# Attention state of a linear-attention + gated-FFN kernel: read-out in four 64x64 array tiles, update by single heads in column tiles directly behind AV

## The chip, the cores and the metric

The kernel runs on one core of a Trainium2 chip. The metric is device time in microseconds (us), the median of a kernel's runs.

Names used below: PE is the TensorE matmul engine, DVE is VectorE, ACT is ScalarE, POOL is GpSimd (it issues most loads), SP is SyncE. A matmul's "tile" is the part of the PE array that it uses, written rows*columns.

## The reference

Four batches, eight heads, 768 positions, head size 64. Each head keeps a 64x64 state that decays by its own factor `lam`.

```python
for b in range(nb):                      # blocks along the sequence
    intra = einsum('bhic,bhjc->bhij', qb, kb) * Dmask      # scores, masked by powers of lam
    intra = einsum('bhij,bhjd->bhid', intra, vb)           # "AV"
    inter = einsum('bhid,bhde->bhie', qb * lam_pow, kv_state)   # state read-out
    out[:, :, sl] = intra + inter
    kv_state = lam_block * kv_state + einsum('bhsd,bhse->bhde', kb * rev_pow, vb)   # state update
x = out as (tokens, 512)
y = (sigmoid(x @ w_gate) * (x @ w_val)) @ w_out            # 512 -> 1536 -> 512
```

## The kernel before

It takes the sequence in six steps of 128 positions. In each step PE makes 12 FFN *units* (four gate matmuls `gp` and four value matmuls `vp` each) and then four blocks of output matmuls (`po`). The attention of the next step is threaded in behind those units: scores `sp`, masked by DVE into `MT`; then the read-out and AV, both summed into `op`; `op` is copied to `XT`, which the next gate and value matmuls read. ACT makes the sigmoid `sg`, DVE the product `ht`, and PE's `po` reads `ht`.

The attention's state `Sb` is held as block-diagonal 128x128 matrices, one per batch and head pair, so that one full-array matmul serves two heads. Half of each is zeros.

```python
Sb = stp.tile([128, B, HP, 128], BF16)               # HP = 4 head pairs

def piece_kd(n, hs):                                  # scale K for the update, on ACT
    for h in hs:
        nc.scalar.mul(KD[n][:, :, h, :], T_["k", n][:, :, h, :], kds[:, h:h + 1])

def piece_a(n, bs):
    for b in bs:
        OP[n, b] = ps_at.tile([128, HP, C], FP32)
        for hp in range(HP if n > 0 else 0):          # read-out, full array, 16 a step
            nc.tensor.matmul(OP[n, b][:, hp, :], lhsT=Sb[:, b, hp, :], rhs=QS[n, b][:, hp, :], ...)
    for b in bs:                                      # AV, 128x64 column tiles, 32 a step
        for hp in range(HP):
            for u in range(2):
                us = slice(u * 64, (u + 1) * 64)
                nc.tensor.matmul(OP[n, b][us, hp, :], lhsT=T_["v", n][:, b, 2 * hp + u, :],
                                 rhs=MT[n, b][:, u, hp, :], ...)

def piece_c(n, hps):                                  # update, full array, two calls of 8 a step
    for hp in hps:
        cp = ps_at.tile([128, B, 128], FP32)
        for b in range(B):
            nc.tensor.matmul(cp[:, b, :], lhsT=KD[n][:, b, 2 * hp:2 * hp + 2, :],
                             rhs=T_["v", n][:, b, 2 * hp:2 * hp + 2, :], ...)
        for u in range(2):                            # only the diagonal blocks are used
            us = slice(u * 64, (u + 1) * 64)
            ...                                       # Sb = dec * Sb + cp, 64x256 each, on DVE
# ... behind units 0 and 1 of steps 2, 3, 4; in step 1 directly behind AV
more[0] = [pair(piece_c, n, 0)]
more[1] = [pair(piece_c, n, 1)]
```

The first step works the same way while the weights are still being loaded.

## Time and profile before

| | before |
|---|---|
| time, median of runs | 232.66 us (232.62 to 232.94) |
| span in the profile | 231.2 us |
| PE busy | 96% |
| first gate matmul | 16.52 us |
| step period (read-out to read-out) | 35.53 us |

How to read it: PE has almost no room left, so only two things can shorten the kernel: a shorter sequence of matmuls, or a gap in it that closes. The page of the profile says both in three lines (span; busy time, share and instruction count of each engine; shares of the chain of work that ended last, where "issue" is time in which an engine waited for nothing that the profile shows and a q behind a name is that engine's queue).

```profile
span 231.2 us, 3734 instructions
PE 221.5 (96%) x1483; PEld 110.6 (48%) x1508; DVE 109.5 (47%) x183; ACT 92.8 (40%) x175; POOL 47.0 (20%) x55
...
PE 78%; DMA 13%; DVE 3%; POOL 3%; issue 2%; POOLq 0%
```

The groups that the change touches, by line and shape (busy us, mean ns of one, then idle time before them). The full-array read-out and update, the DVE update, and ACT's scaling of K:

```profile
L98 ACT ACTIVATE kd<-kb,kds 128x256 bf16<-128x256 bf16 x40 | 17.8, 497 | 0.0
L260 DVE SCALAR_TENSOR_TENSOR Sb<-Sb,dec,cp 64x256 bf16<-64x256 bf16 x32 | 15.3, 478 | 0.8
L252 PE MATMUL cp<-vb,kd 128*128 128x128 bf16 x80 | 5.9, 219 | 0.1
L230 PE MATMUL op<-QS,Sb 128*128 128x128 bf16 x80 | 5.3, 219 | 0.0
```

PE's busy figures mislead here, because the records of pipelined matmuls overlap (219 ns each for 128x128, started 56 ns apart). Starts are what count. The timeline of PE (columns: start us, busy us, engine, line, operation, tensors, array tile, shape, count, and in brackets the idle time before with what ended it) gives the wait for a slice of WV at 38.29; the attention of step 1 (41.55 to 44.55) with a stop of PE at 49.25; and the attention of step 3 (112.86 to 114.87) with its update behind units 0 and 1:

```profile
10.85 0.62 PE L178 MATMUL tq<-ident,qb 128*128 128x128 bf16 x8 [0.39 <-DMA qb<-in_q_dram]
...
16.52 1.02 PE L273 MATMUL gp<-XT,WG 128*128 128x512 bf16 x4 [0.34 <-DVE XT L246]
...
38.29 1.04 PE L279 MATMUL vp<-XT,WV 128*128 128x512 bf16 x4 [0.33 <-DMA WV<-in_moe_w_val_dram]
...
41.55 1.06 PE L230 MATMUL op<-QS,Sb 128*128 128x128 bf16 x16
42.53 1.08 PE L236 MATMUL op<-MT,vb 128*64 128x128 bf16 x32
43.55 1.07 PE L252 MATMUL cp<-vb,kd 128*128 128x128 bf16 x16
44.55 1.02 PE L273 MATMUL gp<-XT,WG 128*128 128x512 bf16 x3
...
49.25 1.02 PE L279 MATMUL vp<-XT,WV 128*128 128x512 bf16 x4 [0.22 <-DVE ht L282]
...
112.86 1.06 PE L230 MATMUL op<-QS,Sb 128*128 128x128 bf16 x16
113.85 1.08 PE L236 MATMUL op<-MT,vb 128*64 128x128 bf16 x32
114.87 10.53 PE L290 MATMUL po<-WO,ht 128*128 128x512 bf16 x47
...
126.97 0.61 PE L252 MATMUL cp<-vb,kd 128*128 128x128 bf16 x8
```

Differences of starts in step 3: read-out 0.99 us, AV 1.02 us. An update of eight matmuls, from its start to the next gate matmul, takes 0.44 us (126.97 to 127.41), twice per step. Counts such as x47 instead of x48, or x3 instead of x4, are records missing from the trace, not missing work.

The DVE updates cost PE more than their matmuls. The chain of waits around unit 4 of step 3 (start us, us, what), before:

```profile
130.61 0.88 PE vp L279 x4
...
131.51 0.48 DVE Sb L260
...
132.01 0.49 DVE Sb L260
...
132.53 0.70 DVE ht L282
...
133.27 1.02 PE gp L273 x4
```

DVE is still updating the state when the value product of the last unit is ready; `ht` comes late, its PSUM tile comes free late, and the next gate matmul starts 1.09 us after the last value group (132.18 to 133.27) instead of the usual 0.86. So 0.23 us are lost in each of steps 2, 3 and 4.

### The profile page before, as it was taken

Reading aid. Unit: us, or ns where it says so; the run is one execution under the profiler, and the core shown is the slowest. Engines: PE = TensorE matmul, PEld = TensorE weight load, DVE = VectorE, ACT = ScalarE, POOL = GpSimd, SP = SyncE. Lnnn points to the kernel's source line nnn. Section 1 sums busy time; section 2 is a strip of 40 time slices with the busy share of each in tenths; the row PEclk is TensorE's granted clock in tenths of the full one; section 3 lists DMA queues with packets and bytes.
Section 4 is the critical chain, followed back from the end, with each engine's and each line's share of the span. In section 5 each row is a group of like instructions: output and inputs, shape, how many; then the busy total and the mean of one; then the engine's idle time right before and its main releaser. Section 6 shows DMA issues by size and latency. Waiting matters only on the chain.

```text
span 231.2 us, 3734 instructions
## 1 busy us (share of the span) xinstructions
PE 221.5 (96%) x1483; PEld 110.6 (48%) x1508; DVE 109.5 (47%) x183; ACT 92.8 (40%) x175; POOL 47.0 (20%) x55
## 2 busy tenths in 40 slices
PE   6889999999999999999999999999999999999993
PEld 2544555644444644444644544644544554444442
DVE  3963668971068401978300978400778600333300
ACT  5557347532225823347433327442333342433220
POOL 7977672000530080026000030000000000000000
PEclk9999999999999999999999999999999999999999
DMA  7999999999799889969922967012100002100022
GB/s 114 156 176 195 173 173 176 207 168 174 209 166 164 170 94 189 224 129 114 157 53 108 209 43 52 1 45 94 45 0 0 3 35 101 48 0 0 0 91 93
DMA packets 103473, 25.15 MB, mean 109 GB/s; under 512 B 93600, under 2 KB 100512, under 8 KB 103456
## 3 DMA queue, kind: packets, MB, share of 16 engines
q0 software_dynamic: 80992, 13.90, 77.0%
q1 hardware_dynamic: 22320, 11.01, 18.5%
q8 instruction: 12, 0.20, 0.3%
q14 instruction: 5, 0.04, 0.0%
q10 hardware_dynamic: 144, 0.00, 0.0%
HBM read 28.32 MB, written 6.29 MB: 150 GB/s over the span
## 4 chain that ended last, share of the span: by engine, by line
PE 78%; DMA 13%; DVE 3%; POOL 3%; issue 2%; POOLq 0%
PE po L290 27%; PE vp L279 22%; PE gp L273 21%; DMA WV<-in_moe_w_val_dram 10%; DMA vb<-in_v_dram 3%; PE op L236 2%; PE sp L216 2%; DVE Sb L260 2%; PE op L230 2%; PE cp L252 2%; DVE ht L282 1%; POOL qb L78 1%; POOL vb L78 0%; POOL kb L78 0%; POOL WV L85 0%
## 5 line engine op out<-in xcount | busy, mean ns | idle before, releaser
L282 DVE TENSOR_TENSOR ht<-sg,vp 128x512 bf16<-128x512 bf16 x72 | 49.4, 687 | 102.6 <-PE vp L279 101.0
L279 PE MATMUL vp<-XT,WV 128*128 128x512 bf16 x282 | 73.4, 379 | 1.0 <-DMA WV<-in_moe_w_val_dram 0.3
L273 PE MATMUL gp<-XT,WG 128*128 128x512 bf16 x277 | 72.8, 379 | 0.9 <-DVE XT L246 0.3
L276 ACT ACTIVATE sg<-gp 128x512 bf16<-128x512 f32 x72 | 43.0, 597 | 74.1 <-PE gp L273 72.0
L290 PE MATMUL po<-WO,ht 128*128 128x512 bf16 (+1 forms) x294 | 62.7, 370 | 0.4 <-issue 0.2
L279 PEld LDWEIGHTS <-WV 128*128 128x128 bf16 x288 | 28.0, 98 | 34.8 <-DMA WV<-in_moe_w_val_dram 0.9
L290 PEld LDWEIGHTS <-ht 128*128 128x128 bf16 x300 | 29.0, 98 | 32.5
L273 PEld LDWEIGHTS <-WG 128*128 128x128 bf16 x288 | 26.8, 98 | 31.4 <-issue 1.8
L295 ACT COPY ob<-po 128x512 f32<-128x512 f32 (+1 forms) x24 | 13.9, 578 | 45.7 <-PE po L290 45.7
L224 DVE TENSOR_TENSOR MT<-sp,mask 128x512 bf16<-128x512 f32 x48 | 30.4, 682 | 0.6 <-PE sp L216 0.5
L98 ACT ACTIVATE kd<-kb,kds 128x256 bf16<-128x256 bf16 x40 | 17.8, 497 | 0.0
L260 DVE SCALAR_TENSOR_TENSOR Sb<-Sb,dec,cp 64x256 bf16<-64x256 bf16 x32 | 15.3, 478 | 0.8
L361 POOL COPY gates<-kt 128x1 bf16<-128x1 bf16 x4 | 0.8, 188 | 69.9 <-DMA kt<-kb 69.9
L246 ACT CAST XT<-op 128x512 bf16<-128x512 f32 x21 | 11.0, 596 | 7.1 <-PE op L236 7.0
L78 POOL DMA_DIRECT2D qb<-in_q_dram x8 | 11.5, 1441 | 3.5 <-issue 1.6
L78 POOL DMA_DIRECT2D vb<-in_v_dram x7 | 10.7, 1533 | 2.6 <-issue 1.4
L78 POOL DMA_DIRECT2D kb<-in_k_dram x7 | 10.2, 1459 | 1.5 <-DMA WV<-in_moe_w_val_dram 0.7
L304 PE MATMUL zps<-Sb 128*128 128x512 bf16 x22 | 7.8, 482 | 2.1 <-DVE Sb L123 2.1
L236 PE MATMUL op<-MT,vb 128*64 128x128 bf16 x192 | 7.1, 221 | 0.4 <-DVE MT L224 0.4
L236 PEld LDWEIGHTS <-vb 128*64 128x64 bf16 x192 | 5.7, 109 | 1.6 <-DMA vb<-in_v_dram 0.4
L252 PEld LDWEIGHTS <-kd 128*128 128x128 bf16 x80 | 5.1, 98 | 2.0
L252 PE MATMUL cp<-vb,kd 128*128 128x128 bf16 x80 | 5.9, 219 | 0.1
(42 smaller groups left out, 77.3 us busy)
## 6 DMA issues: line engine op xcount, KB each, us to landing
out_dram<-ob SPq DMA_DIRECT2D x23, 256.0 KB, 2.0
vb<-in_v_dram POOLq DMA_DIRECT2D x5, 512.0 KB, 7.9
kb<-in_k_dram POOLq DMA_DIRECT2D x4, 512.0 KB, 10.6
qb<-in_q_dram POOLq DMA_DIRECT2D x4, 512.0 KB, 12.7
WO<-in_moe_w_out_dram POOLq DMA_DIRECT2D x2, 768.0 KB, 16.7
WG<-in_moe_w_gate_dram POOLq DMA_DIRECT2D x5, 256.0 KB, 9.6
WV<-in_moe_w_val_dram POOLq DMA_DIRECT2D x5, 256.0 KB, 10.2
qb<-in_q_dram POOLq DMA_DIRECT2D x4, 256.0 KB, 8.4
```

What stands on the lines that cost most here:

```text
L78: nc.gpsimd.dma_start(out=T_[c, n][:, b0:b1], in_=src[b0:b1, :, sl, :].rearrange("b h s d -> s (b h) d"))
L98: nc.scalar.mul(KD[n][:, :, h, :], T_["k", n][:, :, h, :], kds[:, h:h + 1])
L224: nc.vector.tensor_tensor(out=MT[n, b][:, u], in0=SP[n, b][u], in1=mask[:, u], op=ALU.mult)
L236: nc.tensor.matmul(OP[n, b][us, hp, :], lhsT=T_["v", n][:, b, 2 * hp + u, :], rhs=MT[n, b][:, u, hp, :], start=(n == 0 and hp == 0), stop= ...
L252: nc.tensor.matmul(cp[:, b, :], lhsT=KD[n][:, b, 2 * hp:2 * hp + 2, :], rhs=T_["v", n][:, b, 2 * hp:2 * hp + 2, :], start=(b == 0), stop=( ...
L260: nc.vector.scalar_tensor_tensor(out=Sb[us, :, hp, us], in0=Sb[us, :, hp, us], scalar=dec[us, hp:hp + 1], in1=cp[us, :, us], op0=ALU.mult, ...
L273: nc.tensor.matmul(gp, lhsT=WG[:, mt, fs], rhs=x[:, mt, :], start=(mt == 0), stop=(mt == NMT - 1))
L276: nc.scalar.activation(sg, gp, AF.Sigmoid)
L279: nc.tensor.matmul(vp, lhsT=WV[:, mt, fs], rhs=x[:, mt, :], start=(mt == 0), stop=(mt == NMT - 1))
L282: nc.vector.tensor_mul(HT[n, ft], sg, vp)
L290: nc.tensor.matmul(po[:, :c1 - c0], lhsT=HT[n, ft][:, tt * 128:(tt + 1) * 128], rhs=WO[:, ft, c0:c1], start=(ft == 0), stop=(ft == NFT - 1))
L295: nc.scalar.copy(ob[:, c0:c1], po[:, :c1 - c0])
```

## The change

Its intent: do no work on zeros. The state is stored compactly (`[128, HP, B, 64]`). The read-out becomes 32 matmuls in 64x64 tiles, four of them side by side. The update becomes 32 matmuls of 128x64 column tiles, with two head pairs in one PSUM tile, and is moved right behind AV, so that the DVE updates run under the 10 us of `po` matmuls.

For four 64x64 tiles to be busy at once, two of them have to take their rows from one half of the partitions and write to the other half (diag below is the run without it). The change gets these by swapping the two heads of every pair in batches 2 and 3. This swap is made where q and k are loaded (from step 1 on), and so it needs swapped copies of two small tables, a swapped choice of mask, and loads split into three.

```diff
+    def swapped(n, b):
+        return n > 0 and b >= NB2
+    def slot(n, b, h):
+        return h ^ 1 if swapped(n, b) else h
+    def half(b, h):
+        return (1 - h % 2) if b >= NB2 else h % 2
 ... (in load)
+            nat = b1 if n == 0 or c == "v" else min(b1, NB2)
+            if b0 < nat:
+                nc.gpsimd.dma_start(out=T_[c, n][:, b0:nat], in_=src[b0:nat, :, sl, :]...)
+            if nat < b1:
+                for u in range(2):
+                    nc.gpsimd.dma_start(out=T_[c, n][:, m:b1, u::2, :],
+                                        in_=src[m:b1, 1 - u::2, sl, :]...)
 ... (in piece_kd: one ACT operation per head and half of the batches, for n > 0)
-            nc.scalar.mul(KD[n][:, :, h, :], T_["k", n][:, :, h, :], kds[:, h:h + 1])
+            for bs in ((0, B),) if n == 0 else ((0, NB2), (NB2, B)):
+                i = slot(n, bs[0], h)
+                nc.scalar.mul(KD[n][:, at, i, :], T_["k", n][:, at, i, :], kds[:, h:h + 1])
 ...
-    Sb = stp.tile([128, B, HP, 128], BF16, tag="Sb", name="Sb")
+    Sb = stp.tile([128, HP, B, 64], BF16, tag="Sb", name="Sb")
 ...
+    lamqs = const.tile([128, HP, C], BF16, tag="lamqs")
+    decs = const.tile([128, HP], FP32, tag="decs")
 ... (in tables_late)
+        for o, i in ((lamqs, lamq), (decs, dec)):
+            for u in range(2):
+                nc.sync.dma_start(out=o[rows_of(u)], in_=i[rows_of(1 - u)])
 ...
+    def piece_i(n):
+        for b in range(B):
+            OP[n, b] = ps_at.tile([128, HP, C], FP32, name="op", tag="ps")
+        for i in range(NB2):
+            for hp in range(HP):
+                for u, b in ((0, i), (1, NB2 - 1 - i), (0, NB2 + i), (1, B - 1 - i)):
+                    w = u if b < NB2 else 1 - u
+                    nc.tensor.matmul(OP[n, b][rows_of(w), hp, :], lhsT=Sb[rows_of(u), hp, b, :],
+                                     rhs=QS[n, b][rows_of(u), hp, :], ...)
 ... (in piece_c)
-            cp = ps_at.tile([128, B, 128], FP32, name="cp", tag="ps")
+        cp = ps_at.tile([128, len(hps), B, 64], FP32, name="cp", tag="ps")
+                for w in range(2):
+                    h = 2 * hp + w
+                    nc.tensor.matmul(cp[rows_of(half(b, h)), i, b, :],
+                                     lhsT=KD[n][:, b, slot(n, b, h), :], rhs=T_["v", n][:, b, h, :], ...)
+            for at, d in ((slice(0, NB2), dec), (slice(NB2, B), decs)):   # 128x128 on DVE
+                nc.vector.scalar_tensor_tensor(out=Sb[:, hp, at, :], in0=Sb[:, hp, at, :], ...)
 ... (in att)
+            piece_i(n)
             piece_a(n, range(B))
             piece_x(n, range(B))
+            if n < NSTEP - 1:
+                piece_c(n, [0, 1])
+                piece_c(n, [2, 3])
 ...
-                more[0] = [pair(piece_c, n, 0)]
-                more[1] = [pair(piece_c, n, 1)]
```

## The prediction

> **What bounds it.** PE: busy 96% of the 231.2 us span at full granted clock (first two parts of the page), 78% of the chain of waits; DMA is 13%, all before 38.3 us (last: 0.33 us of PE idle for the last WV slice). From then on PE is almost gapless, so only what shortens PE's sequence, or an idle gap in it, counts. DVE (47%), ACT (40%) and POOL have room. Per step the timeline of PE shows: state read-out 16 matmuls, 0.98 us; AV 32 matmuls, about 1.02 us; state update 2x8 matmuls, 0.44 us each; the other 33 us are gate, value and output matmuls, which the change doesn't touch.
>
> **Read-out (5 steps).** Single matmul starts in the trace: 128x128 full-array ones follow every 56 ns; AV's column tiles and the scores' row tiles start in pairs 3 ns apart, pairs every 56 ns. So tiles do run side by side. Four 64x64 tiles: 32 matmuls in 8 groups, about 8x56 = 0.45 us instead of 0.89. A change of array shape costs: from the last full-array matmul's slot to the first tiled one and back I read 93-95 ns each time. The Trainium skill (TensorEngine Tiling, Key Properties) says that a mode switch drains the array; this trace agrees. The change adds one switch per step (full to 64x64) and about 25 ns for a first weight load. Net saving about 0.32 us a step.
>
> **Update (5 steps).** 16x56 = 0.89 us becomes 16 pairs with 64 moving columns: 28 ns a pair if weight loads hide. The trace shows column-tile weight loads 27 ns apart at AV's start, so hiding is marginal; I estimate 32 ns, 0.50 us. Right behind AV it needs no new switch, except at step 0 (+0.19 us). Saving 0.39 us at steps 2-4, 0.2 at step 0 (which the WV wait at 38 us mostly swallows).
>
> **DVE waits.** State updates behind units 0 and 1 delay ht and stop PE 0.23 us at unit 4 of steps 2, 3, 4 (97.7, 133.3, 168.8 us) and 0.22-0.38 us at 49.2. They move under the 10 us of output matmuls, and 8x507 ns becomes, by my estimate, 8x370 ns. Those four stops should go: 0.9-1.05 us.
>
> **Costs.** The scaling of K becomes 16 ACT operations per step instead of 8 (pitch 0.40 us each becomes about 0.30, as the 128-column table exponentials show): a unit's ACT work reaches 1.7 of 1.73 us, still hidden, except at step 1: there read-out waits for the mask products (all four op banks are wanted at once; DVE ends them at 42.5), and the second update tile waits for ACT's backlog. Step 1 gains nothing and may lose 0.2 us. Loads of k and q split in three: POOL issues longer[...]. The queue is saturated then (DMA share 9 tenths), so I expect 0, at worst 0.8 us. Four small table copies: nothing.
>
> **Sum.** 4x0.32 + 3x0.39 + 1.0 - 0.1 = about 3.4 us: 232.7 becomes 229.3 us, range 228.3 to 230.9. Faster by over 2% (under 228.0) 7%, within 2% 91%, slower 2%.
>
> **What would show it.** Read-out stage (first read-out to first AV matmul) near 0.55 us, groups of four starts; update 32 matmuls near 0.5 us; no PE stop at unit 4 of steps 2-4; state-update DVE ops near 370 ns pitch; step period from 35.53 us (112.86 to 148.40) to about 34.6; first 38 us unchanged within 0.5.
>
> **What would make it wrong.** Four tiles that don't overlap (read-out stays 0.9; then 230.6); short column-tiled matmuls bound by their weight loads at 55 ns a pair (update stays 0.9; 230.5); the last WV slice landing late; ACT lag stopping sigmoid, hence PE, in units 6 to 9.

## The result, and the profile after

| | before | after |
|---|---|---|
| time, median of runs | 232.66 us (232.62 to 232.94) | 230.25 us (230.21 to 230.28) |
| ratio | | 0.9894, interval 0.9877 to 0.9911 |
| span | 231.2 us | 228.4 us |
| PE busy | 96% | 96% |

A ratio here and below is the mean time of one kernel's fast runs over that of the other's of the same rounds, so it is not quite the ratio of the quoted medians. The kernel became 2.4 us faster, 1.1%, where 3.4 us had been expected. The measured time lies inside the predicted range.

The page after (span; engines; chain):

```profile
span 228.4 us, 4108 instructions
PE 218.3 (96%) x1642; PEld 107.2 (47%) x1668; DVE 100.9 (44%) x177; ACT 98.2 (43%) x207; POOL 57.9 (25%) x73
...
PE 89%; DVE 3%; DMA 3%; issue 2%; POOL 1%; POOLq 0%; DVEq 0%
```

DVE gave up 8.6 us of work and ACT took on 5.4; neither is the bottleneck. The groups after, by line and shape, answer to the four of before:

```profile
L121 ACT ACTIVATE kd<-kb,kds 128x128 bf16<-128x128 bf16 x64 | 20.1, 390 | 0.0
L300 DVE SCALAR_TENSOR_TENSOR Sb<-Sb,dec,cp 128x128 bf16<-128x128 bf16 x16 | 5.5, 342 | 3.2 <-PE cp L291 3.2
...
L291 PE MATMUL cp<-vb,kd 128*64 128x64 bf16 x160 | 3.6, 196 | 0.1
L262 PE MATMUL op<-QS,Sb 64*64 64x128 bf16 x160 | 3.6, 219 | 0.4 <-DVE MT L252 0.4
```

The timeline of PE after, same columns: prologue, step 1, step 3.

```profile
12.09 0.62 PE L206 MATMUL tq<-ident,qb 128*128 128x128 bf16 x8 [1.06 <-DMA qb<-in_q_dram]
...
17.82 1.02 PE L313 MATMUL gp<-XT,WG 128*128 128x512 bf16 x4 [0.34 <-DVE XT L283]
...
42.47 0.40 PE L262 MATMUL op<-QS,Sb 64*64 64x128 bf16 x3
43.25 0.60 PE L262 MATMUL op<-QS,Sb 64*64 64x128 bf16 x29 [0.38 <-DVE MT L252]
43.78 1.08 PE L273 MATMUL op<-MT,vb 128*64 128x128 bf16 x32
44.70 0.93 PE L291 MATMUL cp<-vb,kd 128*64 128x64 bf16 x32
45.81 1.04 PE L313 MATMUL gp<-XT,WG 128*128 128x512 bf16 x3 [0.18 <-DVE XT L283]
...
112.91 0.64 PE L262 MATMUL op<-QS,Sb 64*64 64x128 bf16 x32
113.48 1.08 PE L273 MATMUL op<-MT,vb 128*64 128x128 bf16 x32
114.39 0.67 PE L291 MATMUL cp<-vb,kd 128*64 128x64 bf16 x32
115.00 4.71 PE L330 MATMUL po<-WO,ht 128*128 128x512 bf16 x20
```

Step 3 did what was hoped: read-out 0.57 us (112.91 to 113.48) instead of 0.99, update 0.61 us (114.39 to 115.00, with the switch back to the full array) instead of 2 x 0.44, and no stop at unit 4. Step 1 did not: its read-out is cut in two by a wait for the mask products. And the first gate matmul comes 1.30 us later.

Cutting the two timelines at the same places gives the balance (starts of the first matmul of each stage; differences in us):

| stage | before | after | change |
|---|---|---|---|
| start to first gate matmul | 16.52 | 17.82 | +1.30 |
| first gate to read-out of step 1 | 25.03 | 24.65 | -0.38 |
| read-out of step 1 to its first gate | 3.00 | 3.34 | +0.34 |
| that gate to the first output matmul | 7.29 | 6.92 | -0.37 |
| first output matmul to read-out of step 2 | 25.49 | 25.58 | +0.09 |
| periods, steps 2 to 5 (three) | 3 x 35.53 | 3 x 34.59 | 3 x -0.94 |
| read-out of step 5 to the last output block | 33.10 | 32.68 | -0.42 |
| sum | 217.03 | 214.77 | -2.26 |

The sum is that of the PE timeline; the median time differs by 2.41 us, and the two executions that were profiled (232.94 and 230.23 us; the first is the longest of its four) by 2.71. What lies behind the start of the last matmul varied between the profiled executions from 5.1 to 5.8 us, without a reason that I found. Differences in total time under about 0.5 us are therefore read from the stages, not from the totals. Two stages scatter, too, as each kernel has one profile: the first gate matmul of move_col came 0.36 us later than before, although nothing ahead of it is changed, and the last WV slice landed at 37.67 us in out_swap and at 38.18 in out_swap_x, whose loads are the same.

Two readings explain most of this table without an experiment:

- *Period.* 0.94 us is read-out 0.33 (0.99 minus 0.57, less 0.09 for the added switch of array shape), update 0.39 (AV and update together 1.02 + 0.89 before, 0.91 + 0.61 after) and the stop of 0.23 us at unit 4. The single matmul starts in the trace show why: the 64x64 matmuls start in groups of four, 3 to 4 ns apart, with groups 55 to 56 ns apart; the update's column tiles start in pairs 31.7 ns apart.
- *Step 1.* The read-out took 1.31 us there (42.47 to 43.78), AV 0.92, the update with its waits 1.11.

The second needs the other engines. ACT, timeline after (the scalings of K, a sigmoid between them):

```profile
38.92 1.27 ACT L121 ACTIVATE kd<-kb,kds 128x128 bf16<-128x128 bf16 x4
40.10 0.58 ACT L316 ACTIVATE sg<-gp 128x512 bf16<-128x512 f32 x1
...
43.39 1.27 ACT L121 ACTIVATE kd<-kb,kds 128x128 bf16<-128x128 bf16 x4
```

DVE, timeline after, the product that waits for this sigmoid and the mask products behind it:

```profile
40.71 0.69 DVE L322 TENSOR_TENSOR ht<-sg,vp 128x512 bf16<-128x512 bf16 x1 [1.18 <-PE sp L244]
41.32 2.48 DVE L252 TENSOR_TENSOR MT<-sp,mask 128x512 bf16<-128x512 f32 x4
```

Four half scalings take 1.27 us where two whole ones took 0.91. The sigmoid behind them therefore starts late (40.10, right when they end), `ht` starts at 40.71, and the mask products end near 43.8. The bracket names PE as the releaser of `ht`, but the scores it names had started at 40.09; the sigmoid ended at 40.68 and is the one that came last. The read-out needs all four output tiles at once, and these come free only as DVE finishes with the scores. The last scalings of K begin at 43.39 and keep ACT until about 44.6. Its first copy to `XT`, which frees a PSUM tile, therefore ends only at 45.13, and the second half of the update waits for that: 0.26 us between single starts at 44.92 and 45.18. In later steps the same scalings stand in units with room (ACT is idle 1.1 us before the last sigmoid of step 2).

What needed experiments is the prologue, and the question which part of the change earns the period.

### The profile page after: what moved, and what is told of

The parts are those of the page before. It is cut to its first block, busy times and chain, and to the rows that moved or that the text cites. A ratio compares the mean times of both kernels' runs of the same rounds, so it can differ in the third digit from the quotient of the medians.

```text
span 228.4 us, 4108 instructions
## 1 busy us (share of the span) xinstructions
PE 218.3 (96%) x1642; PEld 107.2 (47%) x1668; DVE 100.9 (44%) x177; ACT 98.2 (43%) x207; POOL 57.9 (25%) x73
## 4 chain that ended last, share of the span: by engine, by line
PE 89%; DVE 3%; DMA 3%; issue 2%; POOL 1%; POOLq 0%; DVEq 0%
PE po L330 27%; PE vp L319 27%; PE gp L313 27%; DMA qb<-in_q_dram 3%; PE sp L244 3%; PE op L273 2%; DVE MT L252 2%; PE op L262 1%; PE cp L291 1%; DVE XT L283 1%; PE tq L206 1%; POOL kb L92 0%; PE tk L206 0%; DVE QS L213 0%; POOL qb L92 0%
## 5 line engine op out<-in xcount | busy, mean ns | idle before, releaser
L316 ACT ACTIVATE sg<-gp 128x512 bf16<-128x512 f32 x72 | 42.9, 596 | 66.0 <-PE gp L313 63.3
L121 ACT ACTIVATE kd<-kb,kds 128x128 bf16<-128x128 bf16 (+1 forms) x72 | 23.7, 402 | 0.0
L98 POOL DMA_DIRECT2D qb<-in_q_dram x10 | 9.0, 916 | 3.1 <-DMA vb<-in_v_dram 2.1
L98 POOL DMA_DIRECT2D kb<-in_k_dram x10 | 8.9, 902 | 1.0 <-DMA WG<-in_moe_w_gate_dram 0.6
L92 POOL DMA_DIRECT2D qb<-in_q_dram x7 | 8.4, 1202 | 0.8 <-POOLq L517 0.8
L92 POOL DMA_DIRECT2D kb<-in_k_dram x6 | 7.0, 1166 | 0.0
L300 DVE SCALAR_TENSOR_TENSOR Sb<-Sb,dec,cp 128x128 bf16<-128x128 bf16 x16 | 5.5, 342 | 3.2 <-PE cp L291 3.2
```

What stands on the lines that cost most here:

```text
L92: nc.gpsimd.dma_start(out=T_[c, n][:, b0:nat], in_=src[b0:nat, :, sl, :].rearrange("b h s d -> s (b h) d"))
L98: nc.gpsimd.dma_start(out=T_[c, n][:, m:b1, u::2, :], in_=src[m:b1, 1 - u::2, sl, :].rearrange("b h s d -> s (b h) d"))
L121: nc.scalar.mul(KD[n][:, at, i, :], T_["k", n][:, at, i, :], kds[:, h:h + 1])
L316: nc.scalar.activation(sg, gp, AF.Sigmoid)
```

## The experiments

Every kernel below gave the right result. "First gate" is the start of the first gate matmul.

### The parts of the step: move_col, diag, out_swap, move_only

**move_col.** The kernel before, with the update alone changed: column tiles, two head pairs per PSUM tile, right behind AV. State and read-out stay block-diagonal.

```diff
-            cp = ps_at.tile([128, B, 128], FP32, name="cp", tag="ps")
+        cp = ps_at.tile([128, len(hps), B, 64], FP32, name="cp", tag="ps")
+                for u in range(2):
+                    nc.tensor.matmul(cp[us, i, b, :], lhsT=KD[n][:, b, 2 * hp + u, :],
+                                     rhs=T_["v", n][:, b, 2 * hp + u, :], ...)
 ... (the DVE updates read the halves of cp; called in att, behind piece_x; step 0's
      two updates both behind unit 5; more[0] and more[1] removed)
```

> Only the second half of the change, in the kernel before: state update by single heads in column tiles, right behind AV (both halves together at step 0), state still block-diagonal, read-out still 16 full-array matmuls, nothing swapped or split. Expected from the trace of the changed kernel: update 32 matmuls in about 0.51 us instead of 0.89 (steps 2 to 4: 3 x 0.39 with no new switch), DVE stops at unit 4 of steps 2 to 4 gone (3 x 0.23), step 0 swallowed by the WV wait, step 1 saves at most 0.4 of update while its DVE updates of 64x256 keep the 0.38 stop: total 1.9 to 2.3 us less, 230.4 to 230.8 us; step period 35.53 becomes 34.91. If the changed form of the read-out were what removed the DVE stops, the period would be 35.15.

Measured: 230.98 us, ratio 0.9920 (0.9908 to 0.9932); period 34.92 us, 0.61 less than before. That is the update's 0.39 plus the stop of 0.23. In step 1 the gate now waits 0.44 us for `XT` on DVE, and the stop at 49.1 stays, since DVE's updates are still eight of 64x256 each. The time lies 0.2 us above the range that I had given; the first gate matmul, at 16.88 instead of 16.52, is more than that, and nothing in the edit explains it (`q` landed late, at 11.21 instead of 10.80).

**move_only.** The kernel before, with the same full-array update, only moved behind AV (and, at step 0, both halves behind unit 5).

```diff
             piece_x(n, range(B))
+            if n < NSTEP - 1:
+                piece_c(n, [0, 1])
+                piece_c(n, [2, 3])
 ...
-                more[0] = [pair(piece_c, n, 0)]
-                more[1] = [pair(piece_c, n, 1)]
```

> The kernel before with the state update moved right behind AV and nothing else: still 16 full-array matmuls, no column tiles. Theory: the DVE stops at unit 4 of steps 2 to 4 go (0.23 us each), PE work unchanged, so the period is 35.30 and the time 232.0 us; with move_col (period 34.91) the column tiles alone are then worth 0.39 us a step. Rival (the shorter update is what ends the stops): period 35.53, 232.7.

Measured: 233.17 us, ratio 1.0017 (1.0004 to 1.0031): the move alone gains nothing, against what I had expected. Its PE timeline in step 3:

```profile
114.68 1.44 PE L252 MATMUL cp<-vb,kd 128*128 128x128 bf16 x16
115.95 1.24 PE L290 MATMUL po<-WO,ht 128*128 128x512 bf16 x5
```

The update takes 1.27 us from its start to the output matmuls, where two times 0.44 would do. It needs four PSUM tiles at once out of a pool of five, right when the four `op` tiles are still being copied out, and waits for them: its starts at 115.24 and 115.73 come 0.05 us after ACT's copies to `XT` end. The stops at unit 4 are gone, and the new wait takes the gain back (period 35.68 us). So in this kernel the move pays only together with the column tiles, which pack two head pairs into one PSUM tile.

**diag and out_swap.** Both have the compact state and the update of the change, but natural inputs: no swapped loads, no table copies, no halved scalings. out_swap makes the cross tiles on the output side instead: for batches 2 and 3 of steps 2 to 5, read-out and AV write to the swapped half of `op`, and the copy to `XT` swaps back in two halves. diag differs from it in two lines and never crosses, so only two tiles at a time can be busy.

```diff
 ... (out_swap)
+    def crossed(n, b):
+        return n >= 2 and b >= NB2
+            w = 1 - u if crossed(n, b) else u
+            nc.tensor.matmul(OP[n, b][rows_of(w), hp, :], lhsT=Sb[rows_of(u), hp, b, :], ...)
+            if crossed(n, b):
+                for u in range(2):
+                    f(XT[n][rows_of(u), :, b, :], OP[n, b][rows_of(1 - u)])
 ... (diag, against out_swap)
-        return n >= 2 and b >= NB2
+        return n >= 99 and b >= NB2
-        if n < 2:
+        if n < 99:
```

> A version without swapped inputs: q, k, mask, tables and state all natural; in batches 2,3 of steps 2 to 5 the four-tile read-out and AV write to the swapped half of the output bank, and the XT eviction swaps back in two 64-partition operations. Step 1 reads out in two diagonal 64x64 tiles, bank by bank. No split loads, no table copies, 8 instead of 16 K scalings, 4 instead of 8 state updates per step. Theory: first gate 16.5, step 1 from read-out to next gate 3.0 us as before the change (3.34 after it), step period 34.6 us as in the changed kernel, since the two more evictions per step fall under the output matmuls: 229.1 us. Rival (split loads and ACT load cost nothing): 229.4, as the version without the copies alone.

> As out_swap, but without the crossing: all steps read out in the two diagonal 64x64 tiles only, 32 matmuls in 16 pairs. Theory (the read-out is bound by how many tiles run side by side): read-out of steps 2 to 5 from first read-out to first AV matmul 1.01 us instead of 0.57, step period 35.04 instead of 34.60, 231.1 us. Rival (halving rows and columns is enough, or the extra evictions of out_swap cost as much): period 34.6, 229.3 us.

Measured: out_swap 229.30 us, ratio 0.9849 (0.9836 to 0.9863), first gate 16.53, step 1 3.04 us, period 34.60. diag 231.08 us, ratio 0.9925 (0.9913 to 0.9938), period 35.04. The PE timeline of diag in step 3:

```profile
112.12 1.08 PE L238 MATMUL op<-QS,Sb 64*64 64x128 bf16 x32
113.13 1.08 PE L261 MATMUL op<-MT,vb 128*64 128x128 bf16 x32
```

The same 32 matmuls in the same tile shape take 1.01 us when two tiles work and 0.57 when four do. The four-fold concurrency is therefore worth 0.44 us a step; without it the read-out in small tiles is no better than the full-array one (0.99, plus a switch). And out_swap shows that the gain of the period does not need the swapped inputs. Against move_col, which has the same update and the full-array read-out, its period is 0.32 us shorter: that is the read-out's share, measured by itself.

**out_swap_x.** out_swap, with the last copy to `XT` of step 1 shared between ACT and DVE, to shorten a wait of 0.44 us there.

```diff
+            if n == 1 and b == B - 1:
+                nc.scalar.copy(XT[n][:, :2, b, :], OP[n, b][:, :2])
+                nc.vector.tensor_copy(XT[n][:, 2:, b, :], OP[n, b][:, 2:])
```

> As out_swap, with the last XT eviction of step 1 shared between ACT and DVE, because the first gate matmul of step 1 waited 0.44 us for DVE there. Expected: that wait falls to about 0.2, 229.05 us; if the next limit is elsewhere, 229.3.

Measured: 229.08 us, ratio 0.9840 (0.9827 to 0.9854). The stage from read-out to gate of step 1 fell from 3.04 to 2.87 us, but 0.4 us came back before it: the last WV slice landed at 38.18 instead of 37.67 us, the value matmuls waited 0.40 us for it, and the read-out of step 1 started at 41.58 against 41.17. Against out_swap this is no clear difference.

### The prologue: before_copy, act_tables, copy_later

My first theory for the 1.30 us was the table copies: four transfers that run in the middle of the loads.

**before_copy.** The kernel before plus the copy of the one larger table (two transfers of 64 KB), to a table that nothing reads.

```diff
+    lamqs = const.tile([128, HP, C], BF16, tag="lamqs")
+    for u in range(2):
+        nc.sync.dma_start(out=lamqs[u * 64:(u + 1) * 64], in_=lamq[(1 - u) * 64:(2 - u) * 64])
```

**act_tables.** The kernel after, with the swapped tables computed by ACT and no copy at all.

```diff
-        for o, i in ((lamqs, lamq), (decs, dec)):
-            for u in range(2):
-                nc.sync.dma_start(out=o[rows_of(u)], in_=i[rows_of(1 - u)])
+    def tables_swapped():
+        for u in range(2):
+            nc.scalar.activation(lnps[rows_of(u), :], lam_bc[rows_of(u), 1 - u::2], AF.Ln)
+        for hp in range(HP):
+            nc.scalar.activation(lamqs[:, hp, :], ip1, AF.Exp, scale=lnps[:, hp:hp + 1])
```

**copy_later.** The kernel after with the two copies in the other order, so that the large one waits on the queue behind the small one, whose source is made late.

```diff
-        for o, i in ((lamqs, lamq), (decs, dec)):
+        for o, i in ((decs, dec), (lamqs, lamq)):
```

> The kernel before, plus the two 64 KB copies of lamq into a table that nobody reads, issued as in the changed kernel. Theory: first gate 16.5 becomes about 17.8; the wait for the last WV slice (0.33 us idle) swallows part, so the time rises by 0.6 to 0.9: 233.3 to 233.6 us. Rival: nothing moves, 232.66.

> The changed kernel, but the swapped tables lamqs and decs are computed by ACT (6 small activations more in a stretch where ACT was idle) instead of being copied by four DMAs. Theory (the 128 KB table copy stands in the way of the q load of step 0): q of batches 2,3 lands near 10.8 us instead of 12.05, the first gate matmul starts at 16.5 instead of 17.82, and after the wait for the last WV slice near 38.3 us about 0.85 us of it is left: 229.4 us. Rival (the prologue is late for another reason: smaller Sb fill, colder clock, plain scatter of landings): first gate stays at 17.8 and the time at 230.25.

> The changed kernel with the two pairs of table copies in the other order on SP's queue, so that the 128 KB copy is issued near 12 us instead of 5.7 us; same bytes, same instructions. Theory: q lands near 10.8 us, first gate 16.5; the copy now delays weight slices instead, so the last WV slice lands up to 0.8 us later than without a copy: 229.5 to 230.2 us. Rival: if it is not where the copy stands in the queue, first gate stays at 17.8 and the time at 230.25.

Measured: before_copy 233.50 us, ratio 1.0026 (1.0014 to 1.0039), first gate 16.68; the forecast of the time came true, its reason did not (17.8 had been expected for the first gate). Its mean is 0.6 us above that of the kernel before in the same rounds, but the execution profiled was the fastest of five (233.18 us, against 232.94 for the profile of before), and in it the first gate is 0.16 and the last matmul 0.14 us late. Where the rest lies no profile shows. act_tables 230.06 us, ratio 0.9886 (0.9871 to 0.9901), first gate 17.40. copy_later 229.82 us, ratio 0.9874 (0.9861 to 0.9888), first gate 17.41.

The theory mostly fell. Without a copy in the way the first gate still comes 0.88 us late; the copy accounts for at most 0.42 of the 1.30 us, not much more than the 0.36 that a single profile was seen to scatter.

### The prologue: before_off32, after_aligned, qkv_off32, split_only

The second theory came from the packet records of the load queue. In the kernel after, the 128-byte packets in which q, k and v arrive took longer than before, although their number and source are the same. What differs is where they land: the two new tables moved every tile behind the constants, so that it started 32 bytes past a multiple of 128 on each partition (64 bytes in act_tables), where it had started on a multiple (addresses of the built programs).

**before_off32.** The kernel before, with 32 unused bytes per partition behind the constants.

```diff
+    pad = const.tile([128, 8], FP32, tag="pad")
 ...
+    nc.vector.memset(pad, 0.0)
```

**after_aligned.** The kernel after, with 96 unused bytes there, which puts the later tiles back on multiples of 128.

```diff
+    pad = const.tile([128, 24], FP32, tag="pad")
 ...
+    nc.vector.memset(pad, 0.0)
```

**split_only.** The kernel before with loads of k and q split as in the change, but not swapped: a test of the load splitting, which I had named as a risk of up to 0.8 us.

```diff
+                for u in range(2):
+                    nc.gpsimd.dma_start(
+                        out=T_[c, n][:, m:b1, u::2, :],
+                        in_=src[m:b1, u::2, sl, :].rearrange("b h s d -> s (b h) d"))
```

**qkv_off32.** before_off32 with a second pad behind the q, k and v tiles, so that only these three are displaced.

```diff
+    pad = const.tile([128, 8], FP32, tag="pad")
 ...
+    pad2 = qkv.tile([128, 24], FP32, tag="pad2", name="pad2", bufs=1)
```

> The kernel before with 32 unused bytes per partition behind the constants and nothing else, so that the q, k, v tiles start 32 bytes past a multiple of 128. Theory (place of the destination): first gate from 16.5 to about 17.4 as in the version with later copies, packets of 128 bytes slower than 32 ns between 8 and 14 us; the WV wait swallows about half: 233.0 to 233.3 us. Rival: 232.7 us, first gate 16.5.

> The changed kernel with 96 unused bytes per partition behind the constants, so that the q, k and v tiles start at a multiple of 128 bytes again, as before the change (the changed kernel's new tables moved them to 32 past one). The three slow-prologue kernels (changed, tables on ACT, copy later) have tiles at 32, 64, 32 past a multiple of 128; the three with first gate near 16.5 to 16.7 (before, before with copy, outputs swapped) at 0. Theory (place of the load's destination): 128-byte packets of 32 ns throughout, first gate at 16.7 to 16.9 (the copy alone cost 0.16 in the kernel before), and after the WV wait 229.5 us. Rival (number of split loads, or chance): first gate 17.8, 230.25 us.

> The kernel before with its k and q loads of batches 2,3 split by even and odd heads as in the change, but not swapped; destinations aligned as before. Theory (place of the destination): first gate stays 16.5, and the last WV slice lands as before within 0.5 us: 232.5 to 233.2 us. Rival (more queued software DMAs slow the first loads): first gate 17.4, 233.0 to 233.5 us.

> As the run before_off32, but a second unused tile behind q, k and v brings everything else back to multiples of 128 bytes, so that only the q, k and v tiles lie 32 bytes off. Theory (destination of the loads): the same as before_off32, first gate 17.37 and 233.5 us. Rival (the place of some other tile, such as QS, MT, XT, kd or the fp32 landing tiles of k): first gate 16.5 to 16.9 and 232.7 us.

Measured, with the mean time of the 128-byte packets that started between 9 and 13 us (worked out from the packet records of each trace):

| kernel | later tiles start at (mod 128 bytes) | packets, ns | first gate, us | time, us | ratio |
|---|---|---|---|---|---|
| before | 0 | 32.0 | 16.52 | 232.66 | 1 |
| before_off32 | 32 | 52.7 | 17.37 | 233.50 | 1.0031 (1.0017 to 1.0045) |
| qkv_off32 | 32 for q, k, v; others 0 | 32.0 | 16.78 | 232.91 | 1.0004 (0.9991 to 1.0016) |
| split_only | 0 | 32.0 | 16.51 | 232.62 | 0.9996 (0.9983 to 1.0008) |
| after | 32 | 42.9 | 17.82 | 230.25 | 0.9894 (0.9877 to 0.9911) |
| copy_later | 32 | 53.0 | 17.41 | 229.82 | 0.9874 (0.9861 to 0.9888) |
| act_tables | 64 | 50.0 | 17.40 | 230.06 | 0.9886 (0.9871 to 0.9901) |
| after_aligned | 0 | 32.0 | 16.56 | 228.95 | 0.9838 (0.9825 to 0.9851) |

(In the kernel after, the table copy runs in this window, and fewer packets started in it: 3924, against 4622 in copy_later and 4873 in before. Its mean is lower than that of copy_later although its prologue is longer.)

The lines of PE's timeline, first before_off32, then after_aligned, then qkv_off32:

```profile
11.75 0.62 PE L179 MATMUL tq<-ident,qb 128*128 128x128 bf16 x8 [0.76 <-DMA qb<-in_q_dram]
17.37 1.02 PE L274 MATMUL gp<-XT,WG 128*128 128x512 bf16 x4 [0.34 <-DVE XT L247]
```

```profile
10.94 0.62 PE L207 MATMUL tq<-ident,qb 128*128 128x128 bf16 x8 [0.86 <-DMA qb<-in_q_dram]
16.56 1.02 PE L314 MATMUL gp<-XT,WG 128*128 128x512 bf16 x4 [0.34 <-DVE XT L284]
```

```profile
11.16 0.62 PE L179 MATMUL tq<-ident,qb 128*128 128x128 bf16 x8 [0.51 <-DMA qb<-in_q_dram]
16.78 1.02 PE L274 MATMUL gp<-XT,WG 128*128 128x512 bf16 x4 [0.34 <-DVE XT L247]
```

What follows:

- The placement is the larger part, shown from both sides. Displacing the kernel before by 32 bytes makes its first gate 0.85 us later; putting the kernel after back on multiples of 128 makes it 1.26 us earlier, back to 0.04 of before. The times say the same over all executions (before_off32 233.47 to 233.50 us in five, after_aligned 228.91 to 229.19 in four), so this is not the scatter of single profiles. In all 14 kernels the packets are slow in this window in exactly the four whose later tiles are all displaced, and in none of the other ten.
- That the slow packets *are* the delay is not shown. In before_off32 they take 65% longer, but only 5% fewer of them start (4621 against 4873): they overlap more. And most of the delay is there before them: the first load of q landed at 8.1 us in the four displaced kernels and at 7.3 to 7.5 in the other ten, although up to 7.5 us the packets took 32 ns in all of them. How the placement delays the landing stays open.
- The copy seems to matter mainly together with it: 0.04 us when all is aligned (after_aligned against before), 0.16 in before_copy, 0.41 when displaced (after against copy_later). With a scatter of 0.36 between single profiles this is a hint, not a proof.
- It is not the place of the q, k and v tiles alone. I had expected qkv_off32 to be as slow as before_off32; its packets took 32.0 ns in the window, and its first gate came 0.26 us late, within the scatter. But it is not free of the effect: from 13.0 to 14.5 us its last 128-byte packets took 40.6 ns in the mean and the 256-byte packets of the weights, whose tiles are not displaced, 51.2, where before has 32.0 and 41.0. The place of another displaced tile must matter for the rest, and which one stays open.
- after_aligned is not quite the old placement: its later tiles start on multiples of 256 bytes, those of the kernel before 128 past one. In the two kernels placed so (after_aligned, and qkv_off32 but for q, k and v) DVE's first two casts of k took 0.43 and 0.51 us, in the other twelve 0.87 to 1.10. Why is open; the first gate waited for q, not for k.
- Also open: why only these first microseconds. From 24 to 36 us some 8200 packets of the same size took 32.0 to 32.2 ns in every kernel, displaced or not.
- Splitting the loads cost nothing that the runs can tell (0.9996, interval 0.9983 to 1.0008).

after_aligned is also the best version together with out_swap_x: 228.95 and 229.08 us, equal within their spread, both 1.6% faster than the kernel before. Of the 1.30 us by which after_aligned beats the kernel after, 0.96 is the earlier last matmul: 1.26 from the prologue and 0.45 in step 1 (2.89 instead of 3.34 us), less 0.73 that came back in two stops ahead of value matmuls (0.25 at 21.1 and 0.48 at 38.6 us; the timelines of PE and of its weight loads name a WV slice as what ended them), where PE now comes earlier than the weights.

## Why the prediction was right or wrong

Inside its range; of its 3.4 us, 2.4 came. That it is inside is partly luck: the 1.30 us of the prologue were in no term of the sum, and part of the room that held them (0.8 us) had been left for the split loads, which cost nothing.

**Right, with the numbers that show it:**

- *PE-bound, almost gapless.* PE was busy 96% after the change, too, and the saving in the period is the sum of what was taken off PE's sequence.
- *Four tiles overlap.* Predicted a read-out near 0.55 us and 0.32 us saved per step; measured 0.57 and 0.33. The Trainium skill (TensorEngine Tiling (Array Packing), Key Properties) says that tiles operate independently and that changing the tiling mode drains the array. The trace agrees with both: four starts 3 to 4 ns apart, and a gap of 90 to 100 ns, beyond the slot of the last matmul, at each change of array shape. diag shows that the concurrency, not the smaller shape, is the gain.
- *Update.* Predicted 32 ns a pair, 0.50 us, 0.39 saved; measured 31.7 ns, 0.51 us for 16 pairs, 0.39 saved. The same page (Restrictions, under Tile-to-Partition Mapping) says that column tiling disables Fast Weight Load; this fits the trace, where two pairs of column-tile weight loads that wait for nothing start about 28 ns apart, against 15 ns for two full-array ones. Whether it is also why a pair with 64 moving columns takes 31.7 ns and not 28 is not shown: no run separates the weight loads from the matmuls.
- *DVE stops.* 0.23 us each at unit 4 of steps 2 to 4 are gone, and -0.37 after step 1's gate. move_only shows a condition that I had not seen: moving the update behind AV removes these stops only to create a wait for PSUM tiles, unless two head pairs share a tile.
- *Splitting the loads.* "I expect 0": split_only says 0.9996.

**Wrong or mis-sized, by terms of the sum:**

1. *"First 38 us unchanged within 0.5"* and *"Four small table copies: nothing."* This is the step that failed. The first gate came 1.30 us later: 0.88 of it stays without the copy and goes with the placement, since the two new tables displaced all later tiles; the other 0.42 came with the copy, and is not much above the scatter of a single profile. 0.29 of it was given back at 38 us, where the WV wait vanished because PE now came later (the slice itself landed at 38.85 instead of 38.24). I had counted what the new operations cost and not what the new tiles would move.
2. *"Step 1 gains nothing and may lose 0.2 us."* Right in its mechanism (ACT's longer scalings, the read-out waiting for the mask products, the second update tile waiting for ACT), small by 0.14: it lost 0.34 us from read-out to gate, and another 0.09 for the switch ahead of it.
3. *"By my estimate 8x370 ns"* for DVE's update: the pitch was 258 ns. This was harmless, since the updates are off the critical path now.

The balance, in us: 3.4 expected; less 1.30 in the prologue; plus 0.29 for the WV wait that vanished; less 0.33 for step 1 (0.34 and the switch of 0.09, of which 0.1 was in the estimate); plus 0.17 for the update of step 0, which the estimate had left to the WV wait; and 0.15 outside the matmuls. That gives 2.4, which is what was measured. The last term is what was left over, not a measurement: between the two profiled executions it is 0.45.

## What to carry to other kernels

A small matmul shape pays for what runs side by side: check that the tiles in flight at once are different parts of the array and together fill it, and that the outputs have a place in PSUM at the moment they are made; without the first the 64x64 read-out gained nothing, without the second the moved update gained nothing. A new constant tile can move the start of every tile behind it, so after any change of buffers compare when the first loads land, and how long their packets take, with the kernel before; an unused pad of 96 bytes per partition was worth as much here as half of the whole change. When a swap is needed somewhere, ask whether it can be made on the side where an engine has room: swapping on the way out needed no new loads, tables or halved scalings.

## What the Trainium skill lacked or had wrong

- *Placement of tiles and load speed (no page has it).* "SBUF — State Buffer", Operand start alignment, is by its own words about legality, not speed, and timed nothing. Here 128-byte load packets took 32.0 ns with all later tiles on multiples of 128 bytes, and 50.0 to 53.0 ns with all of them 32 or 64 bytes off and no table copy in the way; the first gate matmul came 0.85 to 0.89 us later. "DMA: Bandwidth & Descriptors", How a descriptor splits into AXI transactions, says that a descriptor that does not start on a 256-byte boundary fetches unused bytes, which would suggest the destination of the slow packets as the cause; with only q, k and v displaced the packets took 32.0 ns up to 13 us, and later also packets to tiles that had not moved were slow (51.2 against 41.0 ns), so this does not bear that out.
- *Back-to-back gap.* "TensorE: Matmul & The Clock Gate", Back-to-back issue gap, gives a sustained spacing of about 81 ns for 128 moving columns and 131 ns for 512 in a stream of weight load and matmul pairs. The traces have 56 and 216 ns, each matmul with its own weight load; this is what the page's formula for a single matmul gives.
- *Weight loads.* The same page, LDWEIGHTS, gives columns divided by 1.2, so about 53 ns for 64 columns. Here pairs of column-tile matmuls, each matmul with its own 64-column load, followed each other every 31.7 ns. Only the spacing is compared; how long one load takes the trace cannot tell, since the ends of its records are modelled.
- *Size of a mode switch.* "TensorEngine Tiling (Array Packing)", Key Properties, says that a switch drains the array but not what it costs: 90 to 100 ns for each change of array shape in these traces.
